# Landmark values times w_in as eight 64x32 array tiles in two banks, heads grouped by parity, first batch in a new order

## The chip, the cores and the metric

The kernel runs on one core of a Trainium2 chip. The metric is device time in microseconds (us): 896.05 is the median of three executions (895.35, 896.05, 901.98). The profile is of one further execution, which took 899.86.

## The reference, cut to what matters

Nystrom attention over 4 batches, 8 heads, 576 positions and 64 dims per head, with 32 landmarks, and behind it two feed-forward layers with 512 features and 2048 hidden ones:

```python
A  = sm(q, k_lm)            # 576 x 32 for each head
Bm = sm(q_lm, k_lm)         # 32 x 32
C  = sm(q_lm, k)            # 32 x 576
Z  = Bm.T / (norms)
for _ in range(6):
    Z = 2 * Z - Z @ Bm @ Z
attn = A @ Z @ C @ v
x = attn.transpose(0, 2, 1, 3).reshape(B * S, H * D)
h = x @ w_in;  x = (h * sigmoid(h)) @ w_out          # layer 1
h = x @ w_in2; out = (h * tanh(softplus(h))) @ w_out2  # layer 2
```

Inputs are float64 in memory; the kernel turns them into float32 on the chip.

## The kernel before, in words

The kernel never forms `attn`. For each head it makes the 32x64 matrix W = Z C v (the landmark values), multiplies W by that head's 64 rows of `w_in`, and has a 32x2048 matrix U; the hidden values are then h = A U, with the 8 heads' landmarks (8 x 32 = 256) as the contraction. So layer 1's first matmul has a contraction of 256 and not of 512.

- A batch has two units `g` of four heads each. `attn_unit` does the scores and softmaxes of Bm and C, `attn_newton` the six steps for Z, and it ends with the matmuls `wk` (line 441) and the copy into the tile `wt` (line 446), which holds W for the unit. `attn_queries` and `attn_softmax` make A (`ath`, and `atl`, the part that rounding leaves).
- `u_steps(b, jp)` (line 518) makes U for two of the sixteen 128-wide column blocks of `w_in`. A `w_in` tile `wc[j]` holds 128 rows at a time, and that is two heads' 64 rows. The masked `wt` holds two heads block by block, with zeros between (line 450, `own2`), so that one matmul of 128 rows and 64 columns serves two heads. There are eight such matmuls of 128 moving columns in a step, two of them (p = 0, 1) side by side on the columns 0-63 and 64-127 of the array. Each float32 matmul shows as two records in the trace, so a step has 16. The step's result fills one PSUM bank (128x512); batch 0 copies it with ACT (line 541), the others with ACT (546) and then a DVE subtraction (548).
- Eight steps make a batch, so there are 32 in all. For batch 0 they stand among the `ha` matmuls (`h_stream`, line 802), for batch 1 among the `ya` matmuls (`y_stream`, line 818), for batches 2 and 3 among the `h` and `y` matmuls of the batch before or of their own (`u_all`, line 985).
- The order of batches 0 and 1 is set by a planner, `interleave` (line 45): each stream of work yields steps with a cost for each engine, and the step with the lowest score goes next. Its score is its estimated begin, plus `WASTE` times the time for which its later engines would stand idle, plus a delay that is written beside the stream (lines 846 to 866). Engines then run what they were given strictly in that order. The order behind it (batches 2 and 3, layer 2) is that of the code, moved a little by the compiler's scheduler.
- Loads go through one queue of SP, also in order; a load whose buffer isn't free yet holds up those behind it. `rawi` and `rawo` are the raw float64 tiles of `w_in` and `w_out`; POOL, two ACT operations and two DVE operations (595, 599) convert each.
- PSUM has eight banks. `Banks(5, 7)` (line 870) gives the attention of batches 2 and 3, and their U, the banks 5 and 7 in turn; `h` uses 4 and 6, `y` 0 to 3.

## Time and profile before

| | |
|---|---|
| median of three executions | 896.05 us |
| the profiled execution, and its span | 899.86 us, 898.1 us |
| TensorE (PE) busy | 863.3 us, 96% |
| VectorE (DVE) busy | 651.1 us, 73% |
| ScalarE (ACT) busy | 472.7 us, 53% |
| GpSimd (POOL) busy | 293.9 us, 33% |
| U matmuls (line 531), busy | 35.0 us, 512 records |
| mean granted clock of TensorE | 0.982 |

PE is busy nearly throughout. A busy PE is not one at its peak: a record's end is modelled, and records overlap, so that what a group of matmuls costs is read from the start of the group to the start of the next one. The granted clock has two levels, 1.0 (2.4 GHz) and 0.5 (1.2 GHz).

### The profile page before, as it was taken

To read this page: it belongs to the slowest core of one execution; us is meant where nothing else is said; L and a number is where in the kernel's file an instruction comes from. 1 tells how busy PE (TensorE), PEld (TensorE's weight loads), DVE (VectorE), ACT (ScalarE), POOL (GpSimd) and SP (SyncE) were. 2 spreads that over 40 slices of the span, in tenths; PEclk is the share of its full clock that TensorE was granted. 3 is DMA by queue.
4 is the path that set the end of the run, shared out by engine and by line. 5 is a ranking of instruction groups with operands and counts; after the bars stand their busy time and mean duration, and the time that the engine had idled before them with its cause. 6 is when DMAs were issued, how large, how long until landed. Compare 5 with 4: busy or idle time off the path is not lost.

```text
span 898.1 us, 15048 instructions
## 1 busy us (share of the span) xinstructions
PE 863.3 (96%) x5440; PEld 762.3 (85%) x5440; DVE 651.1 (73%) x1265; ACT 472.7 (53%) x1013; POOL 293.9 (33%) x334
## 2 busy tenths in 40 slices
PE   7799989999999998899999999999999999999997
PEld 5567767779998998899899889899999999999896
DVE  3878858676576968742364997787787787797776
ACT  3656546345344646653564555554554554555544
POOL 2211333015343545532433542242242242242221
PEclk8899989999999999999999999999999999999999
DMA  8645663433454576720562210110110110000000
GB/s 230 169 97 169 189 192 101 81 81 88 100 149 101 143 224 222 244 87 17 161 181 68 79 45 1 36 35 1 36 36 1 37 36 1 35 1 1 36 1 35
DMA packets 95354, 79.62 MB, mean 89 GB/s; under 512 B 52528, under 2 KB 80688, under 8 KB 95280
## 3 DMA queue, kind: packets, MB, share of 16 engines
q1 hardware_dynamic: 95280, 78.67, 30.6%
q8 instruction: 42, 0.69, 0.3%
q14 instruction: 32, 0.26, 0.1%
HBM read 60.82 MB, written 17.83 MB: 88 GB/s over the span
## 4 chain that ended last, share of the span: by engine, by line
PE 79%; DVE 8%; DMA 5%; ACT 3%; POOL 2%; issue 2%; SPq 1%; ACTq 0%; DVEq 0%; POOLq 0%
PE hh L608 21%; PE o L1098 20%; PE y L608 14%; PE h L608 7%; PE ya L829 5%; PE u L531 4%; PE ha L628 3%; DMA q<-in_q_dram 2%; PE nw L423 1%; DVE z L1036 1%; DMA w2r<-w2c 1%; DMA k<-in_k_dram 1%; PE cv L374 1%; POOL rawt L590 1%; PE c L307 1%
## 5 line engine op out<-in xcount | busy, mean ns | idle before, releaser
L1042 POOL TENSOR_TENSOR g<-z,g 128x384 fp32r<-128x384 f32 x94 | 96.0, 1022 | 256.0 <-ACT g L1039 253.6
L608 PE MATMUL y<-g,wh 128*128 128x288 f32 x768 | 162.4, 302 | 6.8 <-ACT g L659 2.9
L1098 PE MATMUL o<-wh,g 128*128 128x512 f32 x576 | 165.7, 395 | 2.9 <-ACT g L1039 1.9
L660 POOL TENSOR_TENSOR g<-g,g 128x288 fp32r<-128x288 f32 x96 | 82.4, 858 | 184.9 <-ACT g L659 143.0
L608 PEld LDWEIGHTS y<-g,wh 128*128 128x128 f32 x768 | 124.5, 190 | 12.0 <-ACT g L659 3.1
L608 PE MATMUL hh<-yl,wi2h 128*128 128x384 f32 x384 | 129.6, 337 | 0.0
L608 PE MATMUL hh<-yh,wi2h 128*128 128x384 f32 x384 | 129.2, 336 | 0.0
L608 PE MATMUL hh<-yh,wi2l 128*128 128x384 f32 x384 | 129.1, 336 | 0.0
L1098 PEld LDWEIGHTS o<-wh,g 128*128 128x128 f32 x576 | 106.0, 188 | 23.3 <-ACT g L1039 4.1
L1039 ACT CAST g<-z 128x384 fp32r<-128x384 f32 x96 | 49.3, 514 | 133.6 <-DVE z L1038 133.6
L608 PE MATMUL y<-g,wl 128*128 128x288 f32 x384 | 114.6, 298 | 0.0
L1025 DVE TENSOR_SCALAR e<-hh 128x384 f32<-128x384 f32 x96 | 53.5, 557 | 64.2 <-PE hh L608 63.9
L608 PE MATMUL h<-ath,uw 128*128 128x288 f32 x384 | 95.1, 302 | 0.0
L658 DVE SCALAR_TENSOR_TENSOR g<-th,h 128x288 f32<-128x288 f32 x96 | 43.0, 447 | 55.8 <-ACT th L657 54.3
L1098 PE MATMUL o<-wl,g 128*128 128x512 f32 x288 | 81.7, 391 | 0.0
L1026 ACT ACTIVATE e<-e 128x384 f32<-128x384 f32 x96 | 50.4, 525 | 51.4 <-DVE e L1025 51.2
L608 PEld LDWEIGHTS hh<-yl,wi2h 128*128 128x128 f32 x384 | 72.1, 188 | 3.7
L608 PEld LDWEIGHTS hh<-yh,wi2h 128*128 128x128 f32 x384 | 72.1, 188 | 3.7
L608 PEld LDWEIGHTS y<-g,wl 128*128 128x128 f32 x384 | 73.0, 190 | 0.0
L1036 DVE SCALAR_TENSOR_TENSOR z<-z,r 128x384 f32<-128x384 f32 x96 | 70.0, 729 | 3.3
L608 PEld LDWEIGHTS hh<-yh,wi2l 128*128 128x128 f32 x384 | 72.1, 188 | 0.0
L608 PEld LDWEIGHTS h<-ath,uw 128*128 128x128 f32 x384 | 68.1, 191 | 3.6 <-issue 3.0
(165 smaller groups left out, 1631.7 us busy)
## 6 DMA issues: line engine op xcount, KB each, us to landing
rawi<-in_moe_w_in_dram SPq DMA_DIRECT2D x16, 512.0 KB, 5.6
rawo<-in_moe_w_out_dram SPq DMA_DIRECT2D x16, 512.0 KB, 3.6
rawt<-in_moe_w_in_dram SPq DMA_DIRECT2D x16, 512.0 KB, 4.7
w2c<-ct SPq DMA_DIRECT2D x32, 256.0 KB, 2.6
rawt<-in_moe_w_out_dram SPq DMA_DIRECT2D x16, 512.0 KB, 3.8
w2r<-w2c SPq DMA_DIRECT2D x32, 256.0 KB, 2.8
v<-in_v_dram SPq DMA_DIRECT2D x32, 144.0 KB, 3.1
ysc<-yo SPq DMA_DIRECT2D x32, 144.0 KB, 1.9
```

The lines of the kernel that those rows point to most:

```text
L531: pe.matmul(ub[64 * p : 64 * p + 64, jj, g], wt[:, p].rearrange("a h m -> a (h m)"), wc[2 * jp + jj][:, (2 * g + p) * P : (2 * g + p + 1) ...
L608: pe.matmul(o, a, b_, start=first and i == 0, stop=last and i == n - 1)
L628: pe.matmul(hb[:, :HB], uw[j // 2][:, j % 2, g], ath[0][:, g, hf * HB : (hf + 1) * HB], start=g == 0, stop=g == 1)
L658: dve.scalar_tensor_tensor(g2, th, 1.0, hb[:, :HB], op0=ALU.add, op1=ALU.mult)
L660: eng.tensor_tensor(gl, g2, gh.bitcast(F32), op=ALU.subtract)
L829: pe.matmul(yb[hf, m][:, :HB], wof[j][:, m * P : (m + 1) * P], gst[j // 2][:, j % 2, hf], start=j == 0, stop=j == NF - 1,)
L1025: dve.tensor_scalar(e, h, 20.0, None, op0=ALU.min)
L1026: ins = act.activation(e, e, AF.Exp)
L1036: dve.scalar_tensor_tensor(z, z, -2.0, r, op0=ALU.add, op1=ALU.mult)
L1039: act.copy(gh, z)
L1042: eng.tensor_tensor(gl, z, gh.bitcast(F32), op=ALU.subtract)
L1098: pe.matmul(obank[i][c], a[:, c * P : (c + 1) * P], w, start=j == 0 and k == 0, stop=j == NF - 1 and k == 2,)
```

## The change

1. Heads are grouped by parity: unit g has the heads 0, 2, 4, 6 or 1, 3, 5, 7. The rows of `w_in` of a unit's head h are then the half g (64 partitions) of row block h.
2. `wk` of a unit goes to the 64 partitions of that half in one matmul, without mask; `wt` is a plain copy of 64x128. `own2` is gone, and three memsets with it.
3. `w_in` tiles lie in pairs (`wcp`, 128x2x512). A step of `u_steps` has eight matmuls again, each with 64 rows (a head's dims), 32 columns (its landmarks) and 256 moving columns (both blocks). They have eight different places in the array: two halves of its rows times four quarters of its columns. The halves write to two different PSUM banks.
4. So a step takes two banks, and each copy or subtraction of it is two of 128x256. In batch 0 a step now waits for the copies of the step before (it was the one before that), since banks 6 and 7 serve every step; in batch 1 the steps alternate between banks 3, 7 and 4, 5; in batches 2 and 3 a step takes 5 and 7.
5. `WASTE` and most delays of the planner are other numbers, and planner costs of the steps of U are adapted.

```diff
-WASTE = 1.33
+WASTE = 1.14
...
-        h0 = 4 * g + 2 * p
+        heads = [2 * (2 * p + h2) + g for h2 in range(2)]
...
-        for i in range(n):
-            for h2 in range(2):
-                pe.matmul(wk[64 * h2 : 64 * h2 + 64, i, :P], rv[:, i, w:], bt["bb", i], start=True, stop=True)
+        for i, g in enumerate(gs):
+            pe.matmul(wk[64 * g : 64 * g + 64, i, :P], rv[:, i, w:], bt["bb", i], start=True, stop=True)
...
-            wt = pl.tile([P, 2, 2, M], F32, tag=tag, name=f"wt{b}{g}")
-            dve.tensor_tensor(
-                wt,
-                wk[:, i, :P].rearrange("a (p h m) -> a p h m", p=2, h=2),
-                own2[:, None, :, None].to_broadcast([P, 2, 2, M]),
-                op=ALU.mult,
-            )
+            wt = pl.tile([P, 4, M], F32, tag=tag, name=f"wt{b}{g}")
+            sl = slice(64 * g, 64 * g + 64)
+            dve.tensor_copy(wt[sl].rearrange("a h m -> a (h m)"), wk[sl, i, :P])
...
-            deps += [("wc", 2 * jp), ("wc", 2 * jp + 1), ("ath", 0, 1)] + ([("u", 0, jp - 2)] if jp > 1 else [])
+            deps += [("wc", 2 * jp), ("wc", 2 * jp + 1), ("ath", 0, 1)] + ([("u", 0, jp - 1)] if jp else [])
...
-        yield Step([("pe", 0.9)], deps)
-        ub = atbank(f"u{b}{jp}").rearrange("a (j g f) -> a j g f", j=2, g=2)
-        for g in range(2):
-            wt = units[b, g]["wt"]
-            for jj in range(2):
-                for p in range(2):
-                    pe.matmul(
-                        ub[64 * p : 64 * p + 64, jj, g],
-                        wt[:, p].rearrange("a h m -> a (h m)"),
-                        wc[2 * jp + jj][:, (2 * g + p) * P : (2 * g + p + 1) * P],
-                        start=True,
-                        stop=True,
-                    )
+        yield Step([("pe", 0.5)], deps)
+        ub = [atbank(f"u{b}{jp}{g}") for g in range(2)]
+
+        for h in range(4):
+            for g in range(2):
+                sl = slice(64 * g, 64 * g + 64)
+                pe.matmul(
+                    ub[g][32 * h : 32 * h + 32, : 2 * P].rearrange("a (j f) -> a j f", j=2),
+                    units[b, g]["wt"][sl, h],
+                    wcp[jp][sl, :, h * P : (h + 1) * P],
+                    start=True,
+                    stop=True,
+                )
...
-        act.copy(uh, ub)
-        yield Step([("dve", 0.7)], (), ("u", b, jp))
-        dve.tensor_tensor(ul, ub, uh.bitcast(F32), op=ALU.subtract)
+        for g in range(2):
+            act.copy(uh[:, g].rearrange("a j f -> a (j f)"), ub[g][:, : 2 * P])
+        yield Step([("dve", 0.8)], (), ("u", b, jp))
+        for g in range(2):
+            dve.tensor_tensor(
+                ul[:, g].rearrange("a j f -> a (j f)"),
+                ub[g][:, : 2 * P],
...
-    streams += [(first_unit(0, 0), Banks(0, 1, 2), 0.38), (first_unit(0, 1), Banks(3, 4, 5), 0.05)]
+    streams += [(first_unit(0, 0), Banks(0, 1, 2), 0.44), (first_unit(0, 1), Banks(3, 4, 5), 0.04)]
...
-    streams += [(u_steps(0, jp), Banks(6 + jp % 2), 0.38 + 0.05 * jp) for jp in range(NF // 2)]
+    streams += [(u_steps(0, jp), Banks(6, 7), 0.07 + 0.05 * jp) for jp in range(NF // 2)]
...
-        streams += [(attn_transposes(units[1, g], ti, 4 + ti), Banks(), (0.75, 0.87)[g]) for ti in range(2)]
-        streams += [(second_attention(g), a1, (0.67, 1.15)[g])]
-        streams += [(attn_softmax(units[1, g]), a1, (1.36, 0.66)[g])]
-    streams += [(u_steps(1, jp), Banks((3, 4)[jp % 2]), 1.24) for jp in range(NF // 2)]
+        streams += [(attn_transposes(units[1, g], ti, 4 + ti), Banks(), (0.75, 1.26)[g]) for ti in range(2)]
+        streams += [(second_attention(g), a1, (0.58, 1.08)[g])]
+        streams += [(attn_softmax(units[1, g]), a1, (1.36, 0.11)[g])]
+    streams += [(u_steps(1, jp), Banks(*((3, 7), (4, 5))[jp % 2]), 1.24) for jp in range(NF // 2)]
```

Line numbers of the changed kernel differ by a few: its U matmuls are on line 524, its Newton matmuls on 421, the others within eight lines of the old ones.

The first place where the order moves is PE's, at the end of batch 0's attention: `nw` is a Newton step of unit 0 or 1, `wk` and `u` are as above. Before:

```order
L423 MATMUL nw_574<-rv_565 128x192
L423 MATMUL nw_579<-rv_570 128x192
L423 MATMUL nw_584<-rv_575 128x192
L423 MATMUL nw_589<-rv_580 128x64
L423 MATMUL nw_594<-rv_585 128x64
L441 MATMUL wk_598<-bb_357,rv_590 64x128 x2
L441 MATMUL wk_602<-bb_470,rv_595 64x128 x2
L531 MATMUL u_609<-wc_249,wt_605 64x128 x2
L531 MATMUL u_609<-wc_340,wt_605 64x128 x2
```

And now:

```order
L421 MATMUL nw_573<-rv_563 128x192
L421 MATMUL nw_582<-rv_569 128x64
L421 MATMUL nw_585<-rv_574 128x192
L421 MATMUL nw_597<-rv_586 128x192
L438 MATMUL wk_600<-bb_346,rv_583 64x128
L421 MATMUL nw_609<-rv_598 128x64
L438 MATMUL wk_615<-bb_472,rv_610 64x128
L524 MATMUL u_619<-wc_239,wt_612 32x256
L524 MATMUL u_620<-wc_239,wt_617 32x256
```

The two units' Newton steps ran in turn from first to last; now unit 0 is two steps ahead, and unit 1's last steps stand alone.

The second place is SP's queue of loads while layer 1's second matmul of batch 0 runs; q and k are of batch 1, unit 1, second half. Before:

```order
L576 DMA rawo_1257<-in_moe_w_out_dram 128x1024
L576 DMA rawo_1269<-in_moe_w_out_dram 128x1024
L576 DMA rawo_1295<-in_moe_w_out_dram 128x1024
L203 DMA q_1317<-in_q_dram 96x6x64 x2
L203 DMA k_1323<-in_k_dram 96x6x64 x2
L576 DMA rawo_1328<-in_moe_w_out_dram 128x1024
```

And now:

```order
L577 DMA rawo_1276<-in_moe_w_out_dram 128x1024
L577 DMA rawo_1294<-in_moe_w_out_dram 128x1024
L201 DMA q_1311<-in_q_dram 96x6x64 x2
L577 DMA rawo_1319<-in_moe_w_out_dram 128x1024
L577 DMA rawo_1329<-in_moe_w_out_dram 128x1024
L577 DMA rawo_1347<-in_moe_w_out_dram 128x1024
L201 DMA k_1363<-in_k_dram 96x6x64 x2
```

The load of q stands behind one raw tile fewer, that of k behind two more. On PE the four transposes that need them stood in two pairs (q and k together, five `ya` matmuls, q and k together), ten `ya` matmuls behind the last transpose of the first half; now they stand as q, q, k, k with 5, 10 and 5 `ya` matmuls between, and from the first half's last q transpose, which frees the buffer, to the second half's first one it is 20 `ya` matmuls (it was ten).

The third place is PE's at the end of batch 0's `ya` matmuls, where the last steps of batch 1's U stand (`u17` is step 7; `h1` and `h0` are the first matmuls of the stage behind). Before:

```order
L829 MATMUL ya11_1529<-gs14_1154,wl0_14_1433 128x288
L829 MATMUL ya12_1531<-gs14_1154,wl0_14_1433 128x288
L829 MATMUL ya13_1533<-gs14_1154,wl0_14_1433 128x288
L531 MATMUL u17_1784<-wc14_1015,wt10_1228 64x128 x2
L531 MATMUL u17_1784<-wc15_1042,wt10_1228 64x128 x2
L531 MATMUL u17_1784<-wc14_1015,wt11_1627 64x128 x2
L531 MATMUL u17_1784<-wc15_1042,wt11_1627 64x128 x2
L608 MATMUL h1_1828<-ath1_1241,uw1_0_1646 128x288
```

And now:

```order
L609 MATMUL h1_1852<-ath1_1213,uw1_0_1660 128x288 x2
L609 MATMUL h1_1852<-atl1_1214,uw1_0_1660 128x288
L524 MATMUL u170_1813<-wc7_1018,wt10_1225 32x256
L524 MATMUL u171_1814<-wc7_1018,wt11_1641 32x256
L524 MATMUL u170_1813<-wc7_1018,wt10_1225 32x256
L524 MATMUL u171_1814<-wc7_1018,wt11_1641 32x256
L524 MATMUL u170_1813<-wc7_1018,wt10_1225 32x256
L524 MATMUL u171_1814<-wc7_1018,wt11_1641 32x256
L524 MATMUL u170_1813<-wc7_1018,wt10_1225 32x256
L524 MATMUL u171_1814<-wc7_1018,wt11_1641 32x256
L609 MATMUL h1_1852<-ath1_1213,uw1_0_1660 128x288
L609 MATMUL h0_1836<-ath1_1213,uw1_0_1660 128x288
```

All steps of batch 1's U had three `ya` matmuls behind the step before. Now the last four steps have none left: step 5 follows step 4 directly, and steps 6 and 7 stand among the first `h` matmuls, `h0` right behind them.

## Rows read from the trace of the kernel before

**Rows 1.** The page: busy us of each engine, share of the span, instructions.

```profile
PE 863.3 (96%) x5440; PEld 762.3 (85%) x5440; DVE 651.1 (73%) x1265; ACT 472.7 (53%) x1013; POOL 293.9 (33%) x334
```

**Rows 2.** Windows by stage: stretch, length, busy us of each engine, PEclk, DMA.

```profile
0.00:50.50 50.50, 38.20 (x333) 29.21 (x333) 30.65 (x82) 24.71 (x61) 12.19 (x40) 0.83 0.66 178
50.50:103.40 52.90, 50.65 (x345) 37.61 (x346) 45.00 (x98) 35.14 (x84) 8.22 (x12) 1.00 0.59 164
103.40:193.00 89.60, 86.45 (x485) 64.20 (x484) 62.62 (x116) 41.14 (x84) 21.65 (x21) 0.96 0.42 117
193.00:425.00 232.00, 225.32 (x1834) 209.66 (x1833) 155.01 (x338) 119.04 (x277) 102.18 (x114) 0.99 0.48 138
```

**Rows 3.** Groups of instructions by form: busy us, mean ns | idle before.

```profile
L531 PE MATMUL u<-wc,wt 128*64 128x128 f32 x512 | 35.0, 279 | 0.0
...
L548 DVE TENSOR_TENSOR uw<-u,uw 128x512 fp32r<-128x512 f32 x24 | 16.5, 688 | 13.0 <-ACT uw L546 13.0
L546 ACT CAST uw<-u 128x512 fp32r<-128x512 f32 x24 | 14.0, 583 | 15.6 <-PE u L531 15.6
...
L682 DVE TENSOR_SCALAR yo<-y 128x288 f32<-128x288 f32 x12 | 5.2, 450 | 0.6 <-PE y L608 0.6
L248 ACT COPY kT<-tr 128x288 f32<-128x288 f32 x12 | 4.8, 400 | 4.4 <-PE tr L242 2.9 <-PE tr L246 1.5
```

**Rows 4.** PE's timeline, 144 to 179 us: start, length, instruction, count.

```profile
144.82 7.54 PE L829 MATMUL ya<-gs,wl 128*128 128x288 f32 x30
...
175.92 1.09 PE L531 MATMUL u<-wc,wt 128*64 128x128 f32 x16
176.95 1.72 PE L829 MATMUL ya<-gs,wl 128*128 128x288 f32 x6
178.60 1.09 PE L531 MATMUL u<-wc,wt 128*64 128x128 f32 x16
```

**Rows 5.** PE's timeline of 175.90 to 175.95 us alone: what had started by then.

```profile
175.92 0.33 PE L531 MATMUL u<-wc,wt 128*64 128x128 f32 x2
```

**Rows 6.** Timeline of all engines at the end of batch 0's Newton steps.

```profile
48.07 0.30 PEld L423 LDWEIGHTS nw<-rv 128*128 128x128 f32 x2 [0.31 <-DVE rv L435]
48.11 0.27 ACT L434 COPY rv<-nw 128x128 f32<-128x128 f32 x1 [0.35 <-PE nw L423]
48.41 0.23 DVE L435 TENSOR_TENSOR rv<-nw,rv 128x64 f32<-128x64 f32 x1 [0.39 <-ACT rv L434]
...
50.50 1.09 PE L531 MATMUL u<-wc,wt 128*64 128x128 f32 x16
```

**Rows 7.** PE's timeline where it waits for loads; in brackets the idle time.

```profile
62.92 0.44 PE L246 MATMUL tr<-ident,q 96*128 96x96 f32 x3 [1.59 <-DMA q<-in_q_dram]
...
120.35 5.04 PE L829 MATMUL ya<-gs,wl 128*128 128x288 f32 x20
126.86 0.44 PE L246 MATMUL tr<-ident,q 96*128 96x96 f32 x3 [1.47 <-DMA q<-in_q_dram]
128.61 0.72 PE L246 MATMUL tr<-ident,k 96*128 96x96 f32 x3 [1.32 <-DMA k<-in_k_dram]
```

**Rows 8.** SP's timeline, 98 to 123 us: issues of loads.

```profile
98.01 23.68 SPq L576 DMA_DIRECT2D rawo<-in_moe_w_out_dram  x9
121.74 1.26 SPq L203 DMA_DIRECT2D q<-in_q_dram  x2
```

**Rows 9.** A window of the stretch at half clock behind these waits.

```profile
128.00:134.80 6.80, 6.19 (x19) 4.68 (x20) 1.00 (x2) 0.50 (x2) 1.93 (x3) 0.50 0.54 202
```

**Rows 10.** Timelines: a step's copy and subtraction; PE at the end of the U steps.

```profile
177.06 0.59 ACT L546 CAST uw<-u 128x512 fp32r<-128x512 f32 x1 [1.57 <-PE u L531]
177.68 0.69 DVE L548 TENSOR_TENSOR uw<-u,uw 128x512 fp32r<-128x512 f32 x1 [1.39 <-ACT uw L546]
...
191.98 1.09 PE L531 MATMUL u<-wc,wt 128*64 128x128 f32 x16
...
195.12 0.40 PE L608 MATMUL h<-ath,uw 128*128 128x288 f32 x1
```

More of the change, by code (lines that the diff above doesn't have):

```diff
@@ L123, in nystrom_moe_kernel @@
     sel2 = cp.tile([P, 2], F32, name="sel2")
-    own2 = cp.tile([P, 2], F32, name="own2")
     blk = cp.tile([P, P], F32, name="blk")
     two = cp.tile([P, 1], F32, name="two")
-    for t in (mask2, mask4, sel2, own2, blk):
+    for t in (mask2, mask4, sel2, blk):
         pool.memset(t, 0.0)
@@ L548, in u_steps @@
-        dve.tensor_tensor(ul, ub, uh.bitcast(F32), op=ALU.subtract)
+        for g in range(2):
+            act.copy(uh[:, g].rearrange("a j f -> a (j f)"), ub[g][:, : 2 * P])
+        yield Step([("dve", 0.8)], (), ("u", b, jp))
+        for g in range(2):
+            dve.tensor_tensor(
+                ul[:, g].rearrange("a j f -> a (j f)"),
+                ub[g][:, : 2 * P],
+                uh[:, g].bitcast(F32).rearrange("a j f -> a (j f)"),
+                op=ALU.subtract,
+            )
@@ L608, in mm3, with first_in @@
             pe.matmul(o, a, b_, start=first and i == 0, stop=last and i == n - 1)
-    wc = {}
     wout = {}
+    wcp = {}
+    def first_in(j):
+        if j // 2 not in wcp:
+            wcp[j // 2] = wp.tile([P, 2, 512], F32, tag=f"wc{j // 2}", name=f"wc{j // 2}")
+        return wcp[j // 2][:, j % 2]
     pairs = {}
@@ L627, in h0_matmuls @@
         for g in range(2):
-            pe.matmul(hb[:, :HB], uw[j // 2][:, j % 2, g], ath[0][:, g, hf * HB : (hf + 1) * HB], start=g == 0, stop=g == 1)
+            pe.matmul(hb[:, :HB], uw[j // 2][:, g, j % 2], ath[0][:, g, hf * HB : (hf + 1) * HB], start=g == 0, stop=g == 1)
     def h1_matmuls(hb, b, j, hf):
@@ L772, in out @@
         def out():
-            wc[j] = wp.tile([P, 512], F32, tag=f"wc{j}", name=f"wc{j}")
-            return wc[j]
+            return first_in(j)
         yield from raw_steps(raws.pop(("i", j)), out, (), ("ci", j))
@@ L847, in nystrom_moe_kernel @@
     order = [(1, g, nm, p) for g in range(2) for nm, p in (("q", 0), ("k", 0), ("q", 1), ("k", 1), ("v", 0), ("v", 1))]
-    streams += [(head_load(*it), Banks(), 1.31) for it in order]
-    streams += [(first_unit(0, 0), Banks(0, 1, 2), 0.38), (first_unit(0, 1), Banks(3, 4, 5), 0.05)]
+    streams += [(head_load(*it), Banks(), 1.27) for it in order]
+    streams += [(first_unit(0, 0), Banks(0, 1, 2), 0.44), (first_unit(0, 1), Banks(3, 4, 5), 0.04)]
     for g in range(2):
-        streams += [(queries(units[0, g]), q01, (0.32, 0.25)[g])]
+        streams += [(queries(units[0, g]), q01, (1.05, 0.65)[g])]
@@ L852, in nystrom_moe_kernel @@
         for ti in range(2):
-            streams += [(attn_transposes(units[0, g], ti, 3 * g + ti), Banks(), (1.35, 0.06)[g])]
-    streams += [(u_steps(0, jp), Banks(6 + jp % 2), 0.38 + 0.05 * jp) for jp in range(NF // 2)]
-    streams += [(h_stream(j, hf), Banks(), 0.59 + 0.01 * (2 * j + hf)) for j in range(NF) for hf in range(2)]
-    streams += [(win_stream(j), Banks(), 1.08 + 0 * j) for j in range(NF)]
+            streams += [(attn_transposes(units[0, g], ti, 3 * g + ti), Banks(), (0.63, 0.13)[g])]
@@ L857, in nystrom_moe_kernel @@
+    streams += [(u_steps(0, jp), Banks(6, 7), 0.07 + 0.05 * jp) for jp in range(NF // 2)]
+    streams += [(h_stream(j, hf), Banks(), 0.63 + 0.01 * (2 * j + hf)) for j in range(NF) for hf in range(2)]
+    streams += [(win_stream(j), Banks(), 1.09 + 0 * j) for j in range(NF)]
     streams += [(y_stream(), Banks(), 1.18)]
-    streams += [(wout_stream(j), Banks(), 1.17 + 0.05 * j) for j in range(NF)]
+    streams += [(wout_stream(j), Banks(), 1.36 + 0.02 * j) for j in range(NF)]
     for g in range(2):
-        streams += [(attn_transposes(units[1, g], ti, 4 + ti), Banks(), (0.75, 0.87)[g]) for ti in range(2)]
-        streams += [(second_attention(g), a1, (0.67, 1.15)[g])]
-        streams += [(attn_softmax(units[1, g]), a1, (1.36, 0.66)[g])]
@@ L863, in nystrom_moe_kernel @@
-    streams += [(u_steps(1, jp), Banks((3, 4)[jp % 2]), 1.24) for jp in range(NF // 2)]
-    streams += [(wsplit_stream(j), Banks(), 2.0) for j in range(NF)]
+        streams += [(attn_transposes(units[1, g], ti, 4 + ti), Banks(), (0.75, 1.26)[g]) for ti in range(2)]
+        streams += [(second_attention(g), a1, (0.58, 1.08)[g])]
+        streams += [(attn_softmax(units[1, g]), a1, (1.36, 0.11)[g])]
+    streams += [(u_steps(1, jp), Banks(*((3, 7), (4, 5))[jp % 2]), 1.24) for jp in range(NF // 2)]
@@ L865, in nystrom_moe_kernel @@
+    streams += [(wsplit_stream(j), Banks(), 2.04) for j in range(NF)]
     attn2 = attn_batch(2)
@@ L938, in second_weights @@
                 if which == 0:
-                    hi = wp.tile([P, ND, P], F32R, tag=f"wc{j}", name=f"wi2h{j}")
+                    if j % 2 == 0:
+                        his = wp.tile([P, 2, ND, P], F32R, tag=f"wc{j // 2}", name=f"wi2h{j}")
+                    hi = his[:, j % 2]
                     if j < 11:
```

13 lines of the change are left out of this document (6 added, 7 removed).

## The prediction

> **What bounds the kernel now.** I read the page's busy times first: PE is busy for 96% of the span, the next engine, DVE, for 73% [rows 1]. Then the windows by stage: PE is busy for 38.2 of the first 50.5 us, and from there on for 95 to 97% of each stage [rows 2]. So in the first 50 us latency counts (loads, DVE, the chain of the Newton steps), and behind them nearly every microsecond taken from PE is a microsecond of the kernel, as long as DVE and ACT keep up. The timeline confirms it where U is made for batch 1: three `ya` matmuls (six records) and a step of U follow each other with no idle time, 1.65 us and 1.03 us [rows 4]. All steps of U together keep PE busy for 35.0 us [rows 3], 32 steps of about 1.03 us: that is what the change works on.
>
> **What a step costs, and what it should cost.** A `ya` record streams 288 columns at a pitch of 7.54 us / 30 = 0.251 us [rows 4], so 128 columns take 0.251 x 128 / 288 = 0.112 us and 256 columns 0.223 us. Sixteen records of 128 columns one by one would take 1.79 us; the step takes 1.03 us, so they run two by two: 8 x 0.112 = 0.89, and 0.14 us for entering and leaving it. A window of 0.05 us shows the same: two records have started in it, before either could have streamed its 0.112 us [rows 5]. They are the two places in the array (p = 0, 1); the second pass of a matmul doesn't hold up the other place's first.
>
> The changed step has eight places, each with one matmul of two records of 256 columns. If all eight run at once as the two do now, it takes 2 x 0.223 + 0.14 = 0.59 us, and I add 0.04 us for starting six more places: **0.63 us, 0.40 us less than 1.03; over 32 steps 12.7 us.** No row shows more than two places at once, nor places that share columns and differ in rows, so the price has to be bounded. Below: 0.59 us, two passes and the frame. Above: only two records at a time, 8 x 0.223 + 0.14 = 1.92 us. I take the lower end, since the nearest row [rows 5] shows two places with operands, weights and results of their own that don't hold each other up, and the new ones are of that kind.
>
> **ACT and DVE.** One copy of 512 columns (0.58 us) becomes two of 256, each under the 0.40 us of 288 columns; one subtraction (0.69 us) becomes two, each under the 0.45 us that DVE takes for 288 columns [rows 3]: at most 0.2 us more on either engine for a step. Under the `h` and `y` matmuls of batches 2 and 3 both engines have room (DVE 155 of 232 us, ACT 119) [rows 2], so 16 steps there give PE's full 6.4 us. That such a step needs both banks of the attention is a wait only where an attention matmul follows at once; the order puts `y` matmuls between, so I take nothing for it (up to 1 us if not).
>
> **Batch 1's U (8 steps).** PE gains 3.2 us, but the order leaves the last four steps without `ya` matmuls between. A step's banks come free when the second subtraction ends: now that is 178.37 for a step that ended at 176.95, 1.4 us later [rows 10]. Step 6 needs the banks of step 4, and between lie step 5 and two `h` matmuls (0.63 + 0.26 us), so it waits at least 0.5 us; step 7 has 1.3 us of cover; `h0` shares bank 4 with step 7 and has one matmul, 0.13 us, ahead of it: 1.3 us. That is some 2 us, and up to 5 if splits and transposes stand ahead of the subtractions on DVE. Before, PE went on without idle time there [rows 10]. I take 3 us lost, so batch 1 gives almost nothing.
>
> **First 50 us.** A Newton step's chain is PE, ACT copy, DVE addition, 1.2 us from PE's 48.07 to the next PE step of that unit, and two units in turn fill each other's gaps [rows 6]. Now unit 1's chain stands nearly alone at the end, and four things stand on DVE among its additions (a softmax's row sums, a transpose and two `w_in` conversions): each delays an addition by what exceeds the slack, about 0.6 us for a conversion. The first U comes **1.5 us later**, by my count of DVE's queue (between 1 us earlier and 4 later). Against it three more `w_in` tiles are converted by then, so the `ha` stage behind has less DVE work (45.0 of 52.9 us before [rows 2]) and can follow the faster PE; there 8 steps give 3.2 us. The removed memsets and the two halves of `wk` are worth nothing: loads end the first wait, and `wk` ran two by two.
>
> **Waits for loads.** PE stands for 1.59 us at 62.9 and for 1.47 and 1.32 us at 126.9 and 128.6, each time with a transpose whose q or k is under way [rows 7], and behind the latter two the clock is at half for 6.8 us [rows 9], which costs about 3.4 us of streaming: 7.8 us together. The load of q was issued at 121.74 behind the raw tiles [rows 8]. Now it stands behind one tile fewer and has 20 `ya` matmuls (10 us) to land in where it had 5.04 us; k stands behind two more tiles (9 tiles took 23.68 us, so 5 us), but its transposes come 10 `ya` matmuls and more later. Both waits should go, and with them the low clock. At 62.9 too more work stands ahead. But a new order makes waits of its own, which I can't see: I take 4 us of the 7.8 (0 to 7.8).
>
> **The sum.** 12.7 - 3 - 1.5 + 4 = 12.2 us, from a profiled execution of 899.86 to 887.7; the median of the runs lies 3.8 lower, at 896.05, so **884 us**. Layer 2 is untouched.
>
> **The rivals.**
> 1. *Only two records at a time* (slower). If places that share rows or columns can't stream side by side, a step takes the upper bound, 1.92 us: 0.89 x 32 = 28.5 us more, and with the other terms (3 + 1.5 - 4) about 925 us. For it: no row shows more than two at once. Against: the two that there are show no hold-up. It decides from a step of 1.03 us up. Harder still, the second pass of each matmul could hold up the next place's first: nine turns of 0.223 us and 0.14, 2.15 us a step, 932 us; rows 5 speak against it, since two places start within the window. The Trainium skill ("TensorE: Matmul & The Clock Gate", section "Part 3: Packing small matmuls — row/col tiling") has a rule that would lead to these nine turns, that matmuls begin and end strictly in program order; the trace agrees with it only if the two passes don't stand next to each other. The same section of the Trainium skill reports tiles in sixteen places running at once, which no run here shows. **Chance 0.10**, of which 0.03 for the nine turns.
> 2. *Four at once.* The halves of the rows run side by side, but columns only two by two, because four moving streams are too many: 4 x 0.223 + 0.14 = 1.03 us, no gain on PE. The sum is then 3 + 1.5 - 4 and the copies, 895 to 899. For it: two column streams is all the trace shows. **Chance 0.17.**
> 3. *Eight at once, but the order gives it back*: the start comes 4 us late, loads still stall PE, the end of batch 1 costs 5: 12.7 - 4 - 5 = 3.7, 892 us. **Chance 0.13.**
> 4. *The forecast*, eight at once and most waits gone: 876 to 889. **Chance 0.60.**
>
> **How the numbers follow.** A measurement of this kernel can tell about 1%, 9 us: 887.1 and 905.0 are the bounds. Of the forecast's cases some nine in ten lie under 887: faster 0.54. Same: rivals 2 and 3 and the rest of the forecast, 0.36. Slower: rival 1, 0.10. The likeliest case's own range is 876 to 889. The range leaves out rival 1, and below 874 little (all waits gone, no loss at batch 1's end: 12.7 + 7.8 = 20.5, 875): 874 to 898.
>
> **What would show it.** Right: U's matmuls keep PE busy for about 20 us where it was 35, and from a step's begin to the next matmul it is about 0.6 us; a narrow window shows eight records begun within 0.1 us; no idle time with q and k at 120 to 130 us and no low clock behind. Wrong: a step of 1.0 us (rival 2) or 1.9 (rival 1); PE waiting for `uw` subtractions beyond 3 us around the first `h`; the first U after 54 us; DVE busy throughout the `ha` stage with PE idle beside it.

## The result and the profile after

The changed kernel takes **888.0 us** (median of four executions, 887.53 to 889.02) against 897.18 us for the kernel before (four, 895.35 to 901.98): a ratio of **0.9891, 95% interval 0.9859 to 0.9923**. A second measurement of the same two kernels (`after_again` below) gave 886.3 us against 898.56, 0.9868 (0.9839 to 0.9898). It is faster, by about the 1% that the prediction took as the bound of what can be told. 884 was forecast, with 874 to 898 as the range.

The profiled execution took 887.88 us with a span of 886.1, 12.0 us under that of before (899.86, 898.1). One profiled execution need not lie at its kernel's median: the executions of one program differ, and so does the granted clock in them. Those of `new_u_old_order` below, for example, go from 889.9 us at a mean granted clock of 0.991 to 902.6 us at 0.975. The page's line of busy times, as in [rows 1]: engine, busy us, share of the span, instructions.

```profile
PE 851.9 (96%) x5424; PEld 740.1 (84%) x5424; DVE 648.5 (73%) x1289; ACT 475.5 (54%) x1045; POOL 290.3 (33%) x331
```

PE is as full as before, with 11.4 us less to do; DVE and ACT hardly moved. The forms of [rows 3], in the kernel after: busy us, mean ns of one, then the idle time before.

```profile
L524 PE MATMUL u<-wc,wt 64*32 64x256 f32 x512 | 23.3, 403 | 0.4 <-DVE uw L544 0.4
L544 DVE TENSOR_TENSOR uw<-u,uw 128x256 fp32r<-128x256 f32 x48 | 18.1, 416 | 10.3 <-ACT uw L541 10.3
L541 ACT CAST uw<-u 128x256 fp32r<-128x256 f32 x48 | 15.6, 376 | 10.5 <-PE u L524 10.4
```

U keeps PE busy for 23.3 us instead of 35.0. One record is longer (403 ns, before 279), but more of them run beside each other. A step's two subtractions take 0.83 us where one took 0.69, its two copies 0.75 where one took 0.58. PE's timeline at two steps of batch 1, as in [rows 4]:

```profile
171.15 0.66 PE L524 MATMUL u<-wc,wt 64*32 64x256 f32 x16
171.74 1.72 PE L835 MATMUL ya<-gs,wl 128*128 128x288 f32 x6
173.39 0.66 PE L524 MATMUL u<-wc,wt 64*32 64x256 f32 x16
```

From a step's begin to the next matmul it is 171.74 - 171.15 = 0.59 us; it was 1.03. And a timeline of the 0.06 us from 57.45 to 57.51 alone, as in [rows 5]:

```profile
57.46 0.45 PE L524 MATMUL u<-wc,wt 64*32 64x256 f32 x8
```

Eight records have begun in it, where two had before.

To see where the 12.0 us lie, both programs are cut at the same places: the first U, the first `ya`, the first `y` of batch 2, layer 2's first matmul `hh` and its last `o`. Windows of the kernel after: stretch, length, then busy us and instructions of PE, PEld, DVE, ACT, POOL, and the granted clock (PEclk), DMA share, GB/s.

```profile
0.00:52.16 52.16, 38.89 (x329) 29.21 (x329) 32.75 (x88) 25.86 (x63) 12.79 (x38) 0.78 0.71 193
52.16:102.03 49.87, 49.11 (x346) 33.21 (x346) 40.45 (x90) 34.08 (x89) 7.97 (x12) 0.95 0.49 142
102.03:188.75 86.72, 83.79 (x507) 60.21 (x507) 67.97 (x134) 44.48 (x97) 19.59 (x22) 1.00 0.50 138
188.75:470.54 281.79, 271.35 (x2209) 250.22 (x2207) 180.63 (x397) 152.81 (x366) 123.63 (x140) 0.99 0.49 143
470.54:881.96 411.42, 408.74 (x2042) 367.22 (x2040) 326.20 (x581) 217.86 (x430) 126.30 (x121) 1.00 0.08 23
```

The last three of these stages in the kernel before (the first two stand in [rows 2], 50.50 and 52.90 us):

```profile
103.39:198.24 94.85, 91.70 (x523) 67.84 (x521) 67.25 (x128) 43.44 (x91) 22.22 (x22) 0.96 0.43 119
198.24:485.26 287.02, 276.93 (x2207) 262.19 (x2206) 180.88 (x377) 151.45 (x349) 124.76 (x140) 0.99 0.48 141
485.26:893.96 408.70, 405.81 (x2042) 365.48 (x2040) 326.91 (x581) 217.59 (x430) 126.47 (x121) 1.00 0.08 23
```

Length after less length before, stage by stage: +1.7, -3.0, -8.1, -5.2 and **+2.7 us in layer 2**, whose instructions are the same (its `w_in` tiles lie in pairs now, and at other addresses); -12.0 together (each rounded). In layer 2 PE is busy for 2.9 us more with as many records.

In the second stage the granted clock is 0.95, and it was 1.00 [rows 2]. PE's timeline at the first U, and the window behind it:

```profile
50.53 0.69 PE L421 MATMUL nw<-rv 128*128 128x64 f32 x2 [0.76 <-DVE rv L433]
...
52.16 1.56 PE L524 MATMUL u<-wc,wt 64*32 64x256 f32 x16
53.65 0.74 PE L244 MATMUL tr<-ident,q 96*128 96x96 f32 x3
```

```profile
52.16:56.80 4.64, 4.64 (x41) 2.37 (x41) 4.43 (x6) 1.84 (x6) 1.52 (x2) 0.50 0.35 109
```

Unit 1's last Newton steps, with PE's waits between them, are followed by half clock for 4.6 us of the stage; its first step of U takes 53.65 - 52.16 = 1.49 us. By the price that the prediction uses (half of such a stretch) that is some 2.3 us, an estimate. The stage's window is at 0.93 to 0.96 in all kernels with the new order, and at 0.97 to 1.00 with the old one; that it is the Newton steps' waits that bring it is not shown by an experiment.

The waits for loads [rows 7], in the timeline of PE after:

```profile
124.92 0.47 PE L244 MATMUL tr<-ident,q 96*128 96x96 f32 x3 [1.43 <-DMA q<-in_q_dram]
```

and the window of [rows 9] after:

```profile
128.00:134.80 6.80, 6.80 (x33) 5.33 (x32) 5.42 (x7) 4.47 (x8) 1.30 (x2) 1.00 0.79 209
```

The waits at 62.9 us and for k are gone, that for q has stayed at 1.43 us, and the clock behind it is at full (it was 0.50 for 6.8 us).

Waits are new in two places. At the end of batch 1's U, which answers to [rows 10], PE's timeline has two waits for subtractions, 1.5 us together, and a third that its idle time doesn't show:

```profile
180.13 1.09 PE L524 MATMUL u<-wc,wt 64*32 64x256 f32 x32
...
182.08 0.99 PE L524 MATMUL u<-wc,wt 64*32 64x256 f32 x16 [0.40 <-DVE uw L544]
183.00 0.53 PE L609 MATMUL h<-ath,uw 128*128 128x288 f32 x2
...
185.76 0.40 PE L609 MATMUL h<-ath,uw 128*128 128x288 f32 x1 [1.09 <-DVE uw L544]
```

The step at 182.08 takes 0.92 us, and not 0.59: the wait for its second bank lies inside it.

And at 296 us PE waits with an attention matmul (`cp`) that wants a bank which U has just used:

```profile
293.81 0.66 PE L524 MATMUL u<-wc,wt 64*32 64x256 f32 x16
...
298.60 0.59 PE L356 MATMUL cp<-ident,ce 128*96 128x128 f32 x3 [2.32 <-DVE uw L544]
```

ACT's timeline at that place shows why the bank comes free so late:

```profile
294.83 0.69 ACT L594 ACTIVATE rawt<-rawt 128x512 uint32<-128x512 uint16 x1 [2.09 <-DMA rawt<-in_moe_w_in_dram]
...
296.81 0.63 ACT L541 CAST uw<-u 128x256 fp32r<-128x256 f32 x2
```

U was done at 294.4, but its copies stand behind a conversion that had waited 2.09 us for its raw tile, and the subtractions behind the copies. On DVE one more conversion (0.83 us) stands before them:

```profile
297.38 0.83 DVE L600 SCALAR_TENSOR_TENSOR ct<-rawt 128x512 uint32<-128x512 uint32 x1
298.14 0.74 DVE L544 TENSOR_TENSOR uw<-u,uw 128x256 fp32r<-128x256 f32 x2
```

Behind this idle time the clock is at half, which the window shows in its third figure from the end:

```profile
299.14:302.55 3.41, 3.41 (x17) 3.41 (x16) 0.58 (x2) 1.32 (x3) 0.38 (x1) 0.50 0.70 206
```

The kernel before has two such stretches in this stage, behind waits of 2.6 us for DVE's `yo` and 2.9 us for ACT's `g`; the change has neither:

```profile
349.82:353.23 3.41, 3.41 (x17) 3.36 (x16) 2.46 (x4) 2.63 (x7) 2.30 (x3) 0.50 0.91 224
452.22:455.63 3.41, 3.41 (x16) 3.41 (x16) 1.89 (x5) 1.88 (x4) 1.05 (x1) 0.50 0.92 278
```

### The profile page after: what moved, and what is told of

It reads as the page before. It is cut to its first block, busy times and chain, and to the rows that moved or that the text cites. A ratio compares the mean times of both kernels' runs of the same rounds, so it can differ in the third digit from the quotient of the medians.

```text
span 886.1 us, 15069 instructions
## 1 busy us (share of the span) xinstructions
PE 851.9 (96%) x5424; PEld 740.1 (84%) x5424; DVE 648.5 (73%) x1289; ACT 475.5 (54%) x1045; POOL 290.3 (33%) x331
## 4 chain that ended last, share of the span: by engine, by line
PE 74%; DVE 8%; issue 5%; POOL 4%; ACT 4%; DMA 3%; SPq 1%; POOLq 0%; DVEq 0%; ACTq 0%
PE hh L609 21%; PE o L1106 21%; PE y L609 11%; PE h L609 5%; PE ya L835 5%; PE ha L635 4%; POOL g L667 2%; PE u L524 2%; DMA q<-in_q_dram 2%; PE nw L421 2%; DVE z L1044 1%; PE cv L372 1%; DVE rawt L596 1%; POOL rawt L591 1%; SPq L201 1%
## 5 line engine op out<-in xcount | busy, mean ns | idle before, releaser
L1047 ACT CAST g<-z 128x384 fp32r<-128x384 f32 x96 | 49.3, 514 | 132.2 <-DVE z L1046 132.2
L665 DVE SCALAR_TENSOR_TENSOR g<-th,h 128x288 f32<-128x288 f32 x96 | 42.9, 447 | 50.4 <-ACT th L664 48.1
```

Of the source, the lines that this page charges most:

```text
L665: dve.scalar_tensor_tensor(g2, th, 1.0, hb[:, :HB], op0=ALU.add, op1=ALU.mult)
L1047: act.copy(gh, z)
```

## The experiments

Each was compared with the kernel before measured beside it, whose median lay between 896.3 and 898.6 us. Lengths of stages are worked out as above, from the first records of `u`, `ya`, `y` and `hh` and the last `o` of each profiled execution, which need not lie at the median (the stages of new_u_old_order add up to 10.0 us less than those of before, its median is 1.7 lower):

| kernel | to first u | u to ya | ya to y | y to hh | layer 2 | median, ratio to before |
|---|---|---|---|---|---|---|
| before | 50.5 | 52.9 | 94.8 | 287.0 | 408.7 | |
| the change | 52.2 | 49.9 | 86.7 | 281.8 | 411.4 | 888.0, 0.9891 |
| after_again | 50.7 | 49.9 | 87.1 | 282.1 | 411.4 | 886.3, 0.9868 |
| new_u_old_order | 48.1 | 53.2 | 91.5 | 279.5 | 411.7 | 895.87, 0.9982 |
| new_u_old_order_slot | 50.6 | 53.7 | 92.8 | 282.7 | 408.9 | 893.91, 0.9955 |
| old_u_new_order | 52.6 | 52.9 | 90.1 | 285.0 | 408.7 | 892.48, 0.9934 |
| before_loads_apart | 49.6 | 53.6 | 92.1 | 285.5 | 408.7 | 897.66, 1.0006 |
| attention_after_y | 49.3 | 50.8 | 86.8 | 280.0 | 411.4 | 886.51, 0.9866 |
| slot_back | 51.0 | 49.8 | 87.5 | 281.3 | 408.6 | 883.33, 0.9827 |
| attention_after_y_slot | 48.9 | 50.5 | 87.0 | 278.7 | 408.6 | 883.05, 0.9851 |
| joined | 51.4 | 49.6 | 87.7 | 280.3 | 409.0 | 884.97, 0.9852 |
| before_shifted | 51.0 | 52.3 | 95.5 | 286.5 | 409.7 | 899.87, 1.0007 |
| two_slots | 48.3 | 49.9 | 88.0 | 278.8 | 409.7 | 885.27, 0.9870 |

### Each half of the change alone

**new_u_old_order**, against the change:

```diff
-WASTE = 1.14
+WASTE = 1.33
...
-    streams += [(u_steps(0, jp), Banks(6, 7), 0.07 + 0.05 * jp) for jp in range(NF // 2)]
+    streams += [(u_steps(0, jp), Banks(6, 7), 0.38 + 0.05 * jp) for jp in range(NF // 2)]
...
```

> The changed kernel with the planner's old numbers (WASTE 1.33 and all old delays); the new U step, its banks and the pairs of w_in tiles stay. My theory: the U step is what pays. The trace of the change has 0.59 us from a step's first record to the next matmul at full clock, against 1.03 before, 0.44 x 32 = 14 us of PE; some 5 us of it go to waits for the two banks (2.3 us and a half clock at 296 us, about 1.5 us at batch 1's end). So U alone gives about 9 us: 888 us against 897 for the kernel before (886 to 892), and the new order is worth 0 to 3 us. PE waits for q and k around 121 to 130 us as before, since that order is back. Rival: the order pays, and the U step's gain is lost in waits: then this kernel stays at 895 to 897 us.

895.87 us, ratio 0.9982 (0.9960 to 1.0005): the new U by itself, in the old order, gives nothing that can be told. My theory fell here. Its profile is the fastest of its twelve executions (889.88 us), so the table can't say where the whole gain went. One place shows: the `ha` stage (u to ya) is no shorter than before, though its eight steps are. new_u_old_order_slot, whose profile (894.59) lies near its median, has the same there (53.7). The stage's window in new_u_old_order:

```profile
48.09:101.30 53.21, 48.69 (x350) 32.48 (x350) 44.16 (x99) 35.49 (x91) 8.72 (x12) 1.00 0.56 153
```

PE is busy for 48.69 us (before 50.65), but stands for 4.5 us where it stood for 2.3. The waits in that window: us in all, times, longest.

```profile
PE nw L421 <- DVE rv L433: 2.2, 2, 1.9
PE tr L244 <- DMA q<-in_q_dram: 1.2, 1, 1.2
PE ha L635 <- ACT uf L535: 0.7, 2, 0.5
```

In the old order the `ha` matmuls and what lies between them don't cover batch 1's Newton steps once PE is faster. In later stages this execution is faster (y to hh 279.5 instead of 287.0; 282.7 in new_u_old_order_slot), and layer 2 takes 3.0 us back.

**old_u_new_order**, against the kernel before: all of the change's planner numbers, costs and dependencies, with the old matmuls.

```diff
-WASTE = 1.33
+WASTE = 1.14
...
-        yield Step([("pe", 0.9)], deps)
+        yield Step([("pe", 0.5)], deps)
...
```

> The kernel before (its U step: 16 matmuls of 128 columns in one bank, block-diagonal landmark values) with the new planner numbers and the new step costs and dependencies, so that the order is near that of the change. My theory: U's matmuls take 35 us again, 14 us come back on PE, the waits for two banks go (up to 5 us): 893 to 900 us, against 897 for the kernel before, that is no gain to speak of. Rival (the order pays): 888 to 890 us with the old U step.

892.48 us, 0.9934 (0.9911 to 0.9957): under my 893 to 900, above the rival's 888 to 890. The order alone is worth 5.1 us in the median, the U step alone 1.7, both together 9 to 12: neither half explains the result. In the profile, the order's gain lies in the stage from `ya` to `y` (90.1 us, before 94.8), though this profile (895.13 us) is the slowest of its six executions.

### What a place costs

**places_priced**, against the change (ahead of the real matmuls):

```diff
+        for h in range(4):
+            for g in range(2):
+                r, c = (g, 0, g, 0)[b], (h, h, 0, 0)[b]
+                pe.matmul(
+                    ub[r][32 * c : 32 * c + 32, : 2 * P].rearrange("a (j f) -> a j f", j=2),
+                    units[b, r]["wt"][64 * r : 64 * r + 64, h],
+                    wcp[jp][64 * r : 64 * r + 64, :, h * P : (h + 1) * P],
...
```

> The changed kernel with eight further matmuls of 64x32 by 256 columns ahead of each U step, whose results the real ones overwrite. They lie in eight places in batch 0, in four places (the four columns of one row half, two matmuls each) in batch 1, in two places (two row halves of one column, four matmuls each) in batch 2, in one place in batch 3. My theory: places with rows or columns of their own run side by side, the matmuls of one place one after the other, each two passes of 0.223 us: the step grows from 0.59 us by 0.45, 0.89, 1.79 and 3.57 us, to 1.04, 1.48, 2.38 and 4.16 us in the four batches, and the kernel by 8 x 6.7 = 53.6 us if all of it is on the path: 941 us (932 to 945). Rival: what pays is not the places but the wider matmul (256 columns instead of 128, eight instead of sixteen in a step); then the places don't matter and each set adds 0.45 us or some like amount in every batch, 14 us in all: 902 us. Second rival: the two row halves don't run side by side and only the columns count: then batch 0's set adds 0.89 us, as batch 1's does.

945.1 us (943.65 to 948.22), 1.0526, just above the 932 to 945 that was expected. PE's timeline at one step each of batch 0 (eight places), 1 (four), 2 (two) and 3 (one); L523 are the added matmuls, L534 the real ones:

```profile
69.87 0.66 PE L523 MATMUL u<-wc,wt 64*32 64x256 f32 x16
70.32 0.64 PE L534 MATMUL u<-wc,wt 64*32 64x256 f32 x16
70.89 0.51 PE L645 MATMUL ha<-ath,uf 128*128 128x288 f32 x1
...
175.52 0.83 PE L523 MATMUL u<-wc,wt 64*32 64x256 f32 x9
...
176.97 1.24 PE L845 MATMUL ya<-gs,wl 128*128 128x288 f32 x4
...
288.61 1.70 PE L523 MATMUL u<-wc,wt 64*32 64x256 f32 x14
...
290.89 0.53 PE L619 MATMUL y<-g,wh 128*128 128x288 f32 x2
...
404.74 3.42 PE L523 MATMUL u<-wc,wt 64*32 64x256 f32 x15
...
408.74 0.53 PE L619 MATMUL y<-g,wh 128*128 128x288 f32 x2
```

From the step's begin to the next matmul: 1.02, 1.45, 2.28 and 4.00 us (expected 1.04, 1.48, 2.38, 4.16). Less the 0.59 of the real set, the same eight matmuls cost 0.43, 0.86, 1.69 and 3.41 us in eight, four, two and one place: 0.43 us a turn, and one turn for each matmul that shares its place. Both rivals fall: a wider matmul alone would have cost the same everywhere, and if the row halves took turns, eight places would have cost as much as four. Summed, 8 x 6.39 = 51 us; the kernel grew by some 57, since it also makes waits (one of 5.3 us for a subtraction).

### The stall at 296 us

**attention_after_y**, against the change:

```diff
-        advance(RB)
+        if not made:
+            advance(RB)
...
-        advance(RB)
+        advance(RB * (1 + made))
```

(`made` is true in turns that call `u_all`.)

> The changed kernel; in the turns of batches 1 and 2 that make U for the next batch, the step of the attention that stood right behind U now stands behind the 12 y matmuls (2.1 us). My theory: the 2.3 us for which PE stands at 296 us before an attention matmul, and the half clock behind it from 299.1 us for 3.4 us (1.7 us of work), come from U taking both of the attention's banks. Both go: 884 to 886 us against 888, and no idle time above 1 us on PE at 290 to 300 us with a uw subtraction as its end. Rival: the cause is ACT, which stood before a conversion whose raw tile was late, so that everything behind it is late wherever the attention's step stands: then PE stands for y's operands (g) instead and the time stays at 887 to 889.

886.51 us, 0.9866 (0.9840 to 0.9893). PE's timeline there:

```profile
295.98 0.59 PE L356 MATMUL cp<-ident,ce 128*96 128x128 f32 x3 [1.58 <-DVE uw L544]
```

`cp` still waits for U's subtraction, 1.58 us in place of 2.32, this time without a half clock behind it; below 1 us was expected. Nor is the difference the edit's for certain: without the edit the same wait takes 3.1 us in after_again, 2.2 in slot_back and 1.6 in two_slots. The trace fits two causes together, that the bank is U's and that U's copies and subtractions are late behind conversions on ACT and DVE; no run took away either by itself. In the median there is no difference from the changed kernel that can be told (0.9868 for after_again). Whether both halves of a step could write to one bank, which would take this wait away, was not tried.

### Layer 2

**after_again** was the changed kernel itself.

> The changed kernel itself, once more beside the others of this call, so that they are compared with it under the same conditions. 887 to 889 us, 0.985 to 0.993 of the kernel before; layer 2's matmuls hh<-yh,wi2h again at 340 ns in the mean (336 in the kernel before), since that comes from the program and not from the run.

886.3 us, a little under the 887 to 889 expected, and layer 2 again 411.4: its slowness belongs to the program. The kernels without `own2` have 411.4 to 411.7 in the table, the kernel before and its kin with it 408.7. Two things could do it: `own2`'s slot is gone and tiles behind it lie 32 bytes lower, or the `w_in` tiles lie in pairs. **slot_back**, against the change (with its memset):

```diff
+    own2 = cp.tile([P, 2], F32, name="own2")
     blk = cp.tile([P, P], F32, name="blk")
```

> The changed kernel with the small tile own2 allotted again (its memset to zero too), and nothing reads it. It takes a slot of 32 bytes a partition, so that every tile behind it lies 32 bytes higher, at addresses 32 modulo 64 as in the kernel before, where the change has them at 0 modulo 64. My theory: layer 2 loses 2.7 us against the kernel before (the lead falls from 14.7 to 12.0 us between 485 us and the end) because its operands lie 32 bytes lower. Then hh<-yh,wi2h is at 336 ns again in place of 340, the lead stays as it is at layer 2's begin, and the time is 884 to 886 us against 888. Rival: it is the pairs of w_in tiles, whose rows are 4 kB apart where they were 2 kB: then 340 ns and 888 us stay.

**883.33 us, 0.9827 (0.9798 to 0.9857)**, 3.0 us under after_again, which was measured beside it, and under the 884 to 886 expected. Its window of layer 2:

```profile
469.60:878.21 408.61, 405.69 (x2042) 365.50 (x2040) 326.77 (x581) 217.56 (x430) 126.38 (x121) 1.00 0.08 23
```

The form that grew most there, of layer 2's first matmul, in the change and then in slot_back (busy us, mean ns):

```profile
L609 PE MATMUL hh<-yh,wi2h 128*128 128x384 f32 x384 | 130.4, 339 | 0.0
```

```profile
L610 PE MATMUL hh<-yh,wi2h 128*128 128x384 f32 x384 | 129.2, 336 | 0.0
```

The pairs stayed; the 2.8 us are gone. **before_shifted**, the counter-test on the kernel before:

```diff
     own2 = cp.tile([P, 2], F32, name="own2")
+    gap = cp.tile([P, 2], F32, name="gap")
+    pool.memset(gap, 0.0)
```

> The kernel before with one more small tile (a slot of 32 bytes, set to zero, read by nothing) behind own2: every tile behind it lies 32 bytes higher, at 0 modulo 64. Order, tiles and instructions are otherwise those of before. My theory (address): hh<-yh,wi2h at 338 to 340 ns instead of 336, layer 2 longer by 2 to 3 us, 899.5 to 900.5 us against 897.5. Rival (the pairs): nothing changes, 336 ns and 897 to 898 us.

Layer 2 takes 1.0 us longer, by its window:

```profile
485.34:895.02 409.68, 406.81 (x2042) 366.88 (x2040) 326.62 (x581) 217.81 (x430) 126.28 (x121) 1.00 0.08 23
```

So a shift alone does it, but by less than I had expected; in the whole time (1.0007, 0.9989 to 1.0025) it can't be told. **two_slots**, against the change:

```diff
+    own2 = cp.tile([P, 2], F32, name="own2")
+    gap = cp.tile([P, 2], F32, name="gap")
+    pool.memset(gap, 0.0)
     blk = cp.tile([P, P], F32, name="blk")
```

> The changed kernel with two small tiles ahead of the others in place of own2's one: every tile behind them lies 64 bytes higher than in the change, 32 bytes higher than in the kernel with one slot, and at 0 modulo 64 again. My theory: what counts is the address modulo 64; then layer 2 takes 411.4 us again from its first matmul to its last (408.6 with one slot), hh<-yh,wi2h 340 ns, and the whole kernel 886 to 888.5 us against 883.3 with one slot. Rival: what counts is the distance from certain tiles that don't move, or a longer period: then layer 2 lies elsewhere, from 408.6 to 413 us; the kernel before lost only 1.0 us in layer 2 by the same shift to 0 modulo 64, which speaks for it.

```profile
465.01:874.70 409.69, 406.84 (x2042) 366.86 (x2040) 326.45 (x581) 217.84 (x430) 126.27 (x121) 1.00 0.08 23
```

Layer 2 takes 409.7 us, and not 411.4 (the whole kernel 885.27, under the 886 to 888.5 expected): the address modulo 64, my theory, is not what counts. By the addresses that the compiled programs give, two_slots and before_shifted, one with pairs and one without, have their first `w_in` tile of layer 2 at the same place, 18880, and the same 409.7 us. So do before and slot_back (18848; 408.7 and 408.6); only the change, after_again and their kin begin at 18816, and have 411.4. The time of layer 2 goes by where its tiles lie, and the pairs have no part in it. But a slot doesn't move every tile, as the expectations above have it: of `hh`'s operands the first eleven tiles of `w_in`'s low part (`wi2l`, 206816 the first) and every second tile of `yh` (184032) lie at the same place in all five kernels. So the address of the tiles that move, or their distance from those that stay, could be what counts. Which it is, and why, stays open.

### What is left of the order, and the parts joined

**before_loads_apart**, against the kernel before:

```diff
-    streams += [(wout_stream(j), Banks(), 1.17 + 0.05 * j) for j in range(NF)]
+    streams += [(wout_stream(j), Banks(), 1.36 + 0.02 * j) for j in range(NF)]
...
-        streams += [(attn_transposes(units[1, g], ti, 4 + ti), Banks(), (0.75, 0.87)[g]) for ti in range(2)]
+        streams += [(attn_transposes(units[1, g], ti, 4 + ti), Banks(), (0.75, 1.26)[g]) for ti in range(2)]
```

> The kernel before with two of the new numbers alone: the delay of the second half of batch 1's transposes, 0.87 to 1.26, and that of the w_out conversions, 1.17 + 0.05 j to 1.36 + 0.02 j. They put the transposes of q and k 5 to 10 ya matmuls apart, as in the change; the first 100 us and U stay. My theory: what the new order gave with the old U step (5.1 us, 892.5 against 897.6) is PE's wait for the loads of q and k at 121 to 130 us and the half clock behind it. Then this kernel takes 891 to 894 us against 898, and the clock stays at full between 128 and 135 us. Rival: the order's gain comes from elsewhere (the first 100 us, batch 1's end): 896 to 898.5.

897.66 us, 1.0006 (0.9983 to 1.0028): no gain, so the expectation failed. PE's timeline shows that the mechanism worked, and what took its place:

```profile
124.94 0.47 PE L246 MATMUL tr<-ident,q 96*128 96x96 f32 x3 [0.28 <-DMA q<-in_q_dram]
...
152.01 0.75 PE L829 MATMUL ya<-gs,wl 128*128 128x288 f32 x2 [2.66 <-DVE yo L682]
```

The load's wait is down to 0.28 us, and the clock was at full behind it. But the two numbers moved other work as well: the next turn of `ya` now waits 2.66 us for DVE to empty its banks (`yo`), a wait that old_u_new_order doesn't have. In the profile 2.8 us of the stage are left (92.1 against 94.8), in the median nothing. That the order's 5.1 us are the loads' is therefore not shown by itself; the trace shows only that its gain lies in that stage.

**new_u_old_order_slot**: new_u_old_order with the edit of slot_back.

> The changed kernel's U step with the old order (895.9 us against 897.6 for the kernel before in its call) and with the slot of 32 bytes back. My theory: layer 2's 2.8 us come back here too: 892.5 to 894 us; then the U step by itself, without the moved addresses, is worth 4 to 5 us in the old order, and the rest of its 14 us of PE goes into waits (batch 1's Newton steps in the ha stage, the two banks at 299 us). Rival: in the old order the time is set by something else and stays at 895 to 897.

893.91 us, 0.9955 (0.9937 to 0.9973): in the range expected. Without the moved addresses the U step by itself is worth 3.4 us of the median in the old order (4 to 5 were expected). With `own2`'s slot in each kernel, U alone gives 0.45%, the order alone 0.66% (old_u_new_order) and both together 1.73% (slot_back), more than the sum of the two, 1.11%.

**attention_after_y_slot** has both edits of its name.

> The changed kernel with the slot of 32 bytes back and the attention's step behind the y matmuls in turns that make U (the two edits that measured 3.0 and some 1.5 us, without the third edit of the joined kernel). My theory: the edits add up: 881 to 883.5 us, against 883.3 with the slot alone; PE's wait before the attention matmul near 295 us is 1.6 us or less instead of 2.2 to 3.1. Rival: the attention's step later gives nothing that lasts, 883 to 885.

883.05 us, 0.9851 (0.9816 to 0.9885), the same as slot_back within the intervals: nothing more that can be told. **joined** has a third edit:

```diff
-    streams += [(u_steps(1, jp), Banks(*((3, 7), (4, 5))[jp % 2]), 1.24) for jp in range(NF // 2)]
+    streams += [(u_steps(1, jp), Banks(*((3, 7), (4, 5))[jp % 2]), 0.0) for jp in range(NF // 2)]
```

> Three edits on the changed kernel together: the slot of 32 bytes back, the attention's step behind the y matmuls in turns that make U, and batch 1's U steps with delay 0.0 in place of 1.24, which puts them in pairs (two steps with banks of their own, then three ya matmuls) and leaves one step instead of four behind the last ya matmuls. My theory: 2.7 us from the slot, 1.5 us from the attention's step, 0.5 to 1.5 us from batch 1's end, since only the last step's wait for its subtraction is left in front of the first h: 882 to 885 us, below the changed kernel and the kernel before. Rival: pairs of steps wait for the banks of the pair before (two steps have four subtractions of 0.42 us, 1.7 us, between PE's 1.2 us for the pair and 0.75 us of ya matmuls), and the third edit gives nothing or costs up to 1 us: 884 to 887.

884.97 us, 0.9852 (0.9826 to 0.9878), no better than slot_back. PE's timeline at the end of batch 1's U:

```profile
181.00 0.66 PE L525 MATMUL u<-wc,wt 64*32 64x256 f32 x16
181.59 0.40 PE L610 MATMUL h<-ath,uw 128*128 128x288 f32 x1
...
187.80 0.40 PE L610 MATMUL h<-ath,uw 128*128 128x288 f32 x1 [0.83 <-DVE g L666]
...
189.65 0.40 PE L610 MATMUL y<-g,wh 128*128 128x288 f32 x1 [0.67 <-POOL g L668]
```

U no longer waits for a subtraction, nor does the first `h`. But the first `h` now meets the wait for its own activation (`g`) instead, 0.83 and 0.67 us, and the stage is as long as in slot_back (87.7 and 87.5). Those 1.5 us were not on the path that sets the end of that stage. The simplest kernel that beats both is slot_back.

## Why the prediction was right, step by step

**A step at 0.63 us, 12.7 us in all** [rows 3 to 5]: right, and a little better. It takes 0.59 us, the lower bound; 0.44 x 32 = 14 us. The 0.04 us for starting six more places had no row behind it, and the rows show no such time. The reading that carried it was that of [rows 5]: two places with operands and results of their own don't hold each other up, and eight don't either. Rivals 1 and 2 fall with it (1.92 and 1.03 us a step), and by places_priced for the right reason: two passes of 0.21 us for a turn, the places free of charge. Rival 1's harder form, in which a matmul's second pass holds up the next place, falls too: eight records of a step's sixteen begin within 0.06 us. The Trainium skill ("TensorE: Matmul & The Clock Gate", section "Part 3: Packing small matmuls — row/col tiling") has the rule that matmuls begin and end strictly in program order; with these rows it agrees in the case that the prediction named, that the two passes of a matmul don't stand next to each other.

**ACT and DVE, at most 0.2 us more a step**: right, 0.17 and 0.14.

**No wait for two banks in batches 2 and 3 (up to 1 us)**: mis-sized. One such wait took 2.32 us, and 3.4 us at half clock behind it, which is 1.7 us of work. What I had not counted is ACT's queue: a conversion whose raw tile is late holds U's copies, and so the banks (a conversion on DVE adds to it). The 5.2 us by which the stage of those two batches became shorter hold more than that: the two half clocks of before, 3.4 us by the same price, are gone too, which the sum hadn't.

**Batch 1's end, 3 us lost**: right in kind, too large: 0.40 + 1.09 us at the two places named and 0.33 inside step 6, 1.8 us, near the 2 us that it had counted before it took 3; and in joined, where the waits are gone, nothing is gained.

**First U 1.5 us later** [rows 6]: 1.7 in this pair of profiles. But over the table that time runs from 48.1 to 51.0 us in the old order and from 48.3 to 52.6 in the new: the term is smaller than what one profile can tell. What the step left out is the clock, which is at half behind unit 1's last Newton steps for 4.6 us of the `ha` stage, some 2.3 us.

**Loads, 4 of 7.8 us** [rows 7 to 9]: right in mechanism, somewhat more. Two of three waits and the half clock are gone: 1.59 + 1.32 + 3.4 = 6.3 us by the price that I gave them. "Both waits should go" was wrong for q, which was issued at 120.05 and still came 1.43 us late at 124.92.

**"Layer 2 is untouched"**: this is the step that was wrong. It lost 2.7 us, because a tile of 8 bytes a partition had been removed that no instruction there reads.

**The median lies 3.8 us under the profiled time**: it did for the execution shown of before, and not for the change, whose profile (887.88) lies at its median (888.0). The sum, 887.7, met the profiled time; the 884 missed the median by this offset, which belonged to one execution. That 12.2 came so near to 12.0 is luck in part. The terms as they came out are 14.0 + 6.3 - 1.8 - 1.7 - 4.0 - 2.7, and two of the clock that the prediction hadn't, 3.4 - 2.3: together 11.2 us, with errors of up to 4 us on either side that cancelled.

**Rival 3** (the order gives it back) did not happen in the change, but new_u_old_order shows it in part: there the `ha` stage was no shorter with the faster U, for PE's waits grew. So the premise that nearly every microsecond taken from PE is one of the kernel held for this change only together with its order.

## What to carry to other kernels

Small matmuls in eight places cost one turn together here; count the turns in the fullest place, not the matmuls. The price was a bank for each row half. A step that is made faster may give its time only if the order around it is made anew (0.45% here without it, 1.73% with it), and of a wait removed it is worth asking which wait stands right behind it. When a stage that nobody touched gets slower, compare the mean time of one of its forms first, and then the addresses of its tiles.
